# A fused attention and two-expert-layer kernel: the left tile's matmuls placed among the last steps, late value products in another PSUM bank, and a new written-out order

## The chip, the cores and the metric

The kernel runs on one core of one Trainium2 chip. The time is the device time of one execution in microseconds (us); of the kernel before there are three runs, with a median of 684.05 us (683.52 to 684.1). One further execution was profiled. The core's engines are TensorE (PE, with its weight loads as PEld), VectorE (DVE), ScalarE (ACT), GpSimd (POOL) and SyncE (SP), which issues most DMAs; each takes its instructions in order, and semaphores order them against one another.

## What is computed

Three stages follow one another; the output of each is the input of the next (cut from the reference):

```python
# 1. attention: q, k, v of shape (4, 8, 576, 64), window 64
scores = q @ k^T / sqrt(64); masked to 0 <= i - j < 64; softmax; @ v
x = attn_out.transpose(0, 2, 1, 3).reshape(2304, 512)
# 2. dense layer: w_in (512, 2048), w_out (2048, 512)
h = x @ w_in
g = np.where(h >= 1, h, np.where(h <= -1, 0.0, (h + 1) ** 2 / 4))
x = g @ w_out
# 3. eight experts, one for each token: w1[e] (512, 1024), w2[e] (1024, 512)
logits = x @ w_gate
expert_idx = np.argmax(logits, axis=1)
out[t] = gate_w[t] * (np.maximum(x[t] @ w1[e], 0.0) @ w2[e])   # e = expert_idx[t]
```

gate_w is the largest softmax probability of a token. All is float32.

## The kernel before

A float32 matmul is done as three: each operand is split into a high and a low part (hi, lo), and hi*hi, hi*lo and lo*hi are added up in PSUM. The 2304 tokens are 18 tiles of 128.

**Phase 1** runs through five blocks of 3, 4, 4, 4 and 3 tiles, with 16 steps for each (steps 0 to 79). A step takes 128 of the 2048 hidden columns: layer 1 (`h<-xT,wi`, L590) into an h bank, the clipped square and its split on ScalarE, VectorE and GpSimd (L601 to L614), layer 2 (`acc<-wo`, L634) added up in four acc banks. The attention of later chunks of tokens is done between these steps: scores (`S<-qk`, L388) into S, mask and exponentials, transposes (L458), and value products (`av<-pb,vt`, L473), which `both_parts` places in an acc bank for the first two blocks and in S afterwards. S is one buffer of two banks; h has two banks, each its own buffer. The profile writes down each attention matmul of the order as two records, so that 16 of the order are 32 there.

**Phase 2** (steps 80 to 119) treats one expert, the commonest of the first tile, as the main one and applies it to all tokens, in five blocks of four tiles (two in the last) with eight steps each. L590 and L634 serve here too, with the expert's weights `we`; a relu and its split stand between them (L622, L624). When a block is done, `out_parts` scales each tile by the gate weight (L843 on VectorE or L847 on ScalarE, as the table YO_V says) and stores it (L849). The last block is tiles 16 and 17.

**The left tile.** Tokens of another expert are counted and ranked (L854 to L920), the expert is read into a register, and its weights are loaded in 16 pieces through three buffers and split (`wl<-er`, L819 to L825). Matmuls with small operands (L955) turn ranks into row numbers (`idx`, L961 to L968); GpSimd gathers the rows (`xl<-x2s,idx`, L973). TensorE transposes them (L994), applies layer 1 (`hl`, L1006), transposes the hidden rows after a relu (`hr` L1012, `ht` L1018) and applies layer 2 (`accl`, L1034). ScalarE scales the result (`yl`, L1040), and GpSimd scatters the rows over those that the main expert left in the output (L1042). If more than one left tile were needed, a loop behind would treat the rest; with these inputs it does not run.

**What sets the order.** HEAD is a list of short names, one for each piece of work (ga and gb are the layers of a phase-1 or phase-2 step, qkp and avp scores and value products of a pair of heads, hip and lop the split of the latter, zl, zh and zv loading and splitting a left weight, kg the gather, xa to xl the left tile, yo and yd scaling and storing an output tile). All engines but SyncE get their instructions in the order of this list; SyncE's order is written by hand from the same list. Tables beside it name the engine of splits and scalings that more than one engine can do.

Of the kernel before, what the change touches and what calls it, by code (L numbers as in the profile page):

```python
# [34 lines left out]
PJ_V = (0, 1, 3, 4, 8, 9, 13, 14, 16, 17, 19, 21, 25, 26, 27, 28, 29, 30, 34)  # L35
PS_V = ((15, 0), (17, 0))
# [4 lines left out]
ELO_P = (4, 6, 7, 9, 10, 14, 15)  # L41
LLO_P = (3, 4, 5, 6, 7, 8, 9, 12, 14, 15)
YO_V = ((0, 1), (1, 1), (2, 1), (2, 3), (3, 3), (4, 0), (4, 1))
# [176 lines left out]
def kernel(  # L220
# [409 lines left out]
    def layer2(acc, g, w):  # L630
        hi, lo = g
        for j, (ga, wa) in enumerate(((hi, 0), (hi, 1), (lo, 0))):
            for t, (a, first, last) in enumerate(acc):
                nc.tensor.matmul(  # L634
                    a, ga[:, t * P:t * P + P], w[:, wa],
                    start=(first and j == 0), stop=(last and j == 2),
                )


    def take(r, t, a):  # L640

# [682 lines left out]
```

## Time and profile before

| | |
|---|---|
| median of three runs | 684.05 us |
| the profiled execution | 683.23 us |
| its span, first to last instruction | 681.5 us |
| mean granted TensorE clock | 0.997 of full speed |
| TensorE busy (matmuls) | 668.0 us, 98% |
| VectorE busy | 412.2 us, 60% |
| ScalarE busy | 390.1 us, 57% |
| GpSimd busy | 109.2 us, 16% |

A busy engine is one with an instruction in it; matmuls overlap, so TensorE's 98% says that it hardly ever stands empty, not that it could do no more. How long a group of matmuls takes is read from the start of the group to the start of the next. "Landing" of a DMA is when its data have arrived. The profiled execution's own time is 683.23 us, 1.7 above its span.

### The profile page before, as it was taken

Reading aid. Unit: us, or ns where it says so; the run is one execution under the profiler, and the core shown is the slowest. Engines: PE = TensorE matmul, PEld = TensorE weight load, DVE = VectorE, ACT = ScalarE, POOL = GpSimd, SP = SyncE. Lnnn points to the kernel's source line nnn. Section 1 sums busy time; section 2 is a strip of 40 time slices with the busy share of each in tenths; the row PEclk is TensorE's granted clock in tenths of the full one; section 3 lists DMA queues with packets and bytes.
Section 4 is the critical chain, followed back from the end, with each engine's and each line's share of the span. In section 5 each row is a group of like instructions: output and inputs, shape, how many; then the busy total and the mean of one; then the engine's idle time right before and its main releaser. Section 6 shows DMA issues by size and latency. Waiting matters only on the chain. (4 is left out here: it accounts for less than half of the span.)

```text
span 681.5 us, 11390 instructions
## 1 busy us (share of the span) xinstructions
PE 668.0 (98%) x4159; PEld 554.7 (81%) x4160; DVE 412.2 (60%) x852; ACT 390.1 (57%) x974; POOL 109.2 (16%) x91
## 2 busy tenths in 40 slices
PE   7999999999999999999999999999999999999996
PEld 3788998888888888888888899988888888888884
DVE  6999998433235423344524336889988776776431
ACT  6997888553636576455625344588555654442331
POOL 2432223112100212111111100031110000001320
PEclk9999999999999999999999999999999999999998
DMA  9996324242232333332320224354434222212441
GB/s 340 401 404 247 101 88 115 63 133 45 62 110 59 81 108 98 82 116 49 97 76 1 78 105 181 102 132 124 132 102 123 70 70 62 62 40 75 133 149 43
DMA packets 76797, 79.39 MB, mean 116 GB/s; under 512 B 46167, under 2 KB 51287, under 8 KB 76610
## 3 DMA queue, kind: packets, MB, share of 16 engines
q1 hardware_dynamic: 76578, 78.20, 37.0%
q8 instruction: 33, 0.54, 0.3%
q0 software_dynamic: 160, 0.43, 0.2%
q14 instruction: 26, 0.21, 0.1%
HBM read 53.80 MB, written 14.42 MB: 100 GB/s over the span
## 5 line engine op out<-in xcount | busy, mean ns | idle before, releaser
L590 PE MATMUL h<-xT,wi 128*128 128x512 f32 (+1 forms) x960 | 209.8, 370 | 0.7 <-DVE pb L462 0.6
L590 PEld LDWEIGHTS h<-xT,wi 128*128 128x128 f32 x960 | 174.5, 188 | 26.3 <-DVE pb L462 0.9
L634 PE MATMUL acc<-wo,ghi 128*128 128x512 f32 x576 | 146.2, 394 | 0.0
L634 PEld LDWEIGHTS acc<-wo,ghi 128*128 128x128 f32 x576 | 106.6, 188 | 22.3 <-issue 0.9
L606 DVE SCALAR_TENSOR_TENSOR a<-h,a 128x512 f32<-128x512 f32 (+1 forms) x80 | 50.7, 635 | 92.5 <-ACT a L603 92.3
L590 PE MATMUL h<-xT,we 128*128 128x512 f32 (+1 forms) x480 | 103.1, 368 | 0.0
L601 ACT ACTIVATE a<-h,half 128x512 f32<-128x512 f32 (+1 forms) x80 | 51.8, 648 | 87.9 <-PE h L590 75.7
L590 PEld LDWEIGHTS h<-xT,we 128*128 128x128 f32 x480 | 84.2, 188 | 15.3
L614 POOL TENSOR_TENSOR glo<-a,ghi 128x512 fp32r<-128x512 f32 (+1 forms) x37 | 46.6, 1262 | 255.7 <-ACT ghi L612 223.6
L634 PE MATMUL acc<-wo,glo 128*128 128x512 f32 x288 | 78.5, 390 | 0.0
L634 PE MATMUL acc<-we,ghi 128*128 128x512 f32 x288 | 72.4, 391 | 0.0
L634 PEld LDWEIGHTS acc<-wo,glo 128*128 128x128 f32 x288 | 54.1, 188 | 11.6
L634 PEld LDWEIGHTS acc<-we,ghi 128*128 128x128 f32 x288 | 53.5, 188 | 10.7
L612 ACT ACTIVATE ghi<-a 128x512 fp32r<-128x512 f32 (+1 forms) x80 | 46.2, 585 | 24.4 <-PE acc L634 14.9
L734 DVE TENSOR_TENSOR gpr<-xg,wgb 128x1024 f32<-128x1024 f32 x34 | 44.2, 1301 | 17.3 <-ACT gpr L742 15.9
L726 DVE CUSTOM_DVE_ANT_0 junk<-xg,wgb 128x512 bf16<-128x512 f32 x76 | 54.0, 711 | 0.8
L742 ACT ACTIVATE gpr<-gpr 128x512 f32<-128x512 f32 x68 | 39.9, 586 | 23.2 <-DVE gpr L734 22.7
L622 ACT ACTIVATE ghi<-h 128x512 fp32r<-128x512 f32 (+1 forms) x40 | 22.0, 551 | 47.8 <-PE h L590 37.8
L603 ACT ACTIVATE a<-a 128x512 f32<-128x512 f32 (+1 forms) x80 | 47.0, 589 | 1.1
L614 DVE TENSOR_TENSOR glo<-a,ghi 128x512 fp32r<-128x512 f32 (+1 forms) x43 | 26.7, 625 | 25.4 <-ACT ghi L612 22.3
L634 PE MATMUL acc<-we,glo 128*128 128x512 f32 x144 | 39.2, 389 | 0.0
L624 DVE SCALAR_TENSOR_TENSOR glo<-h,ghi 128x512 fp32r<-128x512 f32 (+1 forms) x40 | 25.2, 632 | 20.4 <-ACT ghi L622 19.9
(167 smaller groups left out, 746.7 us busy)
## 6 DMA issues: line engine op xcount, KB each, us to landing
qk<-in_qq_dram SPq DMA_DIRECT2D x26, 320.0 KB, 3.5
er<-in_w_dram SPq DMA_DIRECT2D x32, 256.0 KB, 2.9
wraw<-in_wi_dram SPq DMA_DIRECT2D x14, 512.0 KB, 7.9
wraw<-in_wo_dram SPq DMA_DIRECT2D x14, 512.0 KB, 8.0
vt<-in_vv_dram SPq DMA_DIRECT2D x26, 256.0 KB, 3.6
xg<-x2s SPq DMA_DIRECT2D x18, 256.0 KB, 2.9
out_dram<-y SPq DMA_DIRECT2D x18, 256.0 KB, 2.4
x2s<-xrow SPq DMA_DIRECT2D x8, 512.0 KB, 3.2
```

Of the source, the lines that this page charges most:

```text
L590: nc.tensor.matmul(h[:, :n], w[:, wa, k * P:k * P + P], x[:, xa, k, o:o + n], start=(i == 0), stop=(i == 3 * KD - 1),)
L601: nc.scalar.activation(a[:, :n], h[:, :n], ACTF.Relu, scale=0.5, bias=half[:, 0:1])
L603: nc.scalar.activation(a[:, :n], a[:, :n], ACTF.Square)
L606: nc.vector.scalar_tensor_tensor(out=a[:, :n], in0=h[:, :n], scalar=1.0, in1=a[:, :n], op0=ALU.max, op1=ALU.min)
L612: nc.scalar.activation(hi[:, :n], a[:, :n], ACTF.Copy)
L614: (nc.gpsimd if pool else nc.vector).tensor_tensor(out=lo[:, :n], in0=a[:, :n], in1=hi[:, :n].bitcast(F32), op=ALU.subtract)
L622: nc.scalar.activation(hi[:, :n], h[:, :n], ACTF.Relu)
L624: nc.vector.scalar_tensor_tensor(out=lo[:, :n], in0=h[:, :n], scalar=0.0, in1=hi[:, :n].bitcast(F32), op0=ALU.max, op1=ALU.subtract,)
L634: nc.tensor.matmul(a, ga[:, t * P:t * P + P], w[:, wa], start=(first and j == 0), stop=(last and j == 2),)
L726: nc.vector.tensor_tensor_reduce(out=junk, in0=xg[t], in1=Z["wgb"][:, e], scale=1.0, scalar=0.0, op0=ALU.mult, op1=ALU.add, accum_out=Z["L ...
L734: nc.vector.tensor_tensor(out=pr, in0=xg[t].unsqueeze(1).to_broadcast([P, 2, DM]), in1=Z["wgb"][:, e:e + 2], op=ALU.mult,)
L742: nc.scalar.activation(pr, pr, ACTF.Copy, accum_out=Z["L"][:, t, e:e + 1])
```

## The change

Three things change together.

1. The left tile's work is no longer behind the last step. Its matmuls stand between the second layers of the last block, and the scatter is issued before the last steps are done. Since the main expert's rows of tiles 16 and 17 are stored later than the scatter, the scatter would be overwritten there. So the rows of these two tiles in the output are cleared beforehand (`ez`), read back behind the scatter into `R` (`xr`, L891 of the changed kernel), and added: a tile's result is `acc * gm + R`, with `gm` the gate weight where the token belongs to the main expert and 0 where it is left (L852, L861). The last tile is added and stored in two halves of 256 columns. The last step's second layer goes tile by tile, with its last tile in two halves.
2. Value products of blocks behind the second are placed in an h bank (`both_parts`).
3. HEAD is a new list, and the engine tables are new (PJ_V, PS_V, ELO_P, LLO_P, YO_V, NRM_P, WLO_P, GLO_P, PB_V, PL_V, PP_A). TensorE has 3587 matmuls instead of 3584.

```diff
-PJ_V = (0, 1, 3, 4, 8, 9, 13, 14, 16, 17, 19, 21, 25, 26, 27, 28, 29, 30, 34)
-PS_V = ((15, 0), (17, 0))
+PJ_V = (3, 4, 5, 7, 8, 11, 18, 19, 21, 23, 27, 29, 31, 32, 33, 34)
+PS_V = ((16, 1), (17, 0), (17, 1))
...
-YO_V = ((0, 1), (1, 1), (2, 1), (2, 3), (3, 3), (4, 0), (4, 1))
+YO_V = ((0, 0), (0, 3), (1, 0), (1, 3), (3, 0))
...
-    "xh1 yd1_119 xj0 xk0 xl0 "
+    "gb116 xj0 ga118 rh117 rv117 ga119 yo3_111 xk0 rh118 gb117 yd3_111 rv118 xl0 rh119 xr1 xr0 gb118 "
+    "rv119 gb119 yo1_119 yo0_119 yd1_119 ye1_119 ys1_119 yd0_119 "
...
-        av = heads(bank("acc" if b <= TPB else "S", "av"))
+        av = heads(bank("acc" if b <= TPB else "h", "av"))
...
-    def layer2(acc, g, w):
+    def layer2(acc, g, w, by_tile):
         hi, lo = g
-        for j, (ga, wa) in enumerate(((hi, 0), (hi, 1), (lo, 0))):
-            for t, (a, first, last) in enumerate(acc):
-                nc.tensor.matmul(
-                    a, ga[:, t * P:t * P + P], w[:, wa],
-                    start=(first and j == 0), stop=(last and j == 2),
-                )
-
+        terms = ((hi, 0), (hi, 1), (lo, 0))
+        part = [(t, slice(0, DM)) for t in range(len(acc))]
+        if by_tile:
+            part[-1:] = [(len(acc) - 1, slice(o, o + DM // 2)) for o in (0, DM // 2)]
+        order = [(q, j) for j in range(3) for q in range(len(part))]
+        for q, j in sorted(order) if by_tile else order:
+            (t, cols), (ga, wa) = part[q], terms[j]
+            a, first, last = acc[t]
+            nc.tensor.matmul(
+                a[:, cols], ga[:, t * P:t * P + P], w[:, wa, cols],
+                start=(first and j == 0),
+                stop=(last and j == 2 and (not by_tile or q != len(acc) - 1)),
+            )
...
     def out_parts(j, t, a):
         ti = j * TB + t
         y = sp.tile([P, DM], F32, tag="st", name="y")
-        if (j, t) in YO_V:
+        if ti == NTILE - 1:
+            r = Z["R"].pop(ti)
+            for o in (0, DM // 2):
+                cols = slice(o, o + DM // 2)
+                nc.vector.scalar_tensor_tensor(
+                    out=y[:, cols], in0=a[:, cols], scalar=Z["gm"][:, t:t + 1], in1=r[:, cols],
+                    op0=ALU.mult, op1=ALU.add,
+                )
+                yield
+                nc.sync.dma_start(out[ti * P:ti * P + P, cols], y[:, cols])
+                yield
+            return
+        if ti in Z["R"]:
+            nc.vector.scalar_tensor_tensor(
+                out=y, in0=a, scalar=Z["gm"][:, t:t + 1], in1=Z["R"].pop(ti), op0=ALU.mult, op1=ALU.add
+            )
+        elif (j, t) in YO_V:
             nc.vector.tensor_scalar(
                 out=y, in0=a, scalar1=Z["GW"][:, ti:ti + 1], scalar2=None, op0=ALU.mult
             )
@@ -848,12 +870,33 @@
         yield
         nc.sync.dma_start(out[ti * P:ti * P + P], y)

+    LAST = TB * (NB2 - 1)
+
+    def clear_last(k):
+        nc.sync.dma_start(out[LAST * P:NT], x2s[NT:NT + 1].to_broadcast([NT - LAST * P, DM]))
+
+    def keep_parts(k):
+        n = NTILE - LAST
+        fl = Z["p2"].tile([P, n], F32, name="fl")
+        nc.vector.tensor_reduce(out=fl, in_=Z["M"][:, LAST:], axis=AX.X, op=ALU.add)
+        gm = Z["gm"] = Z["p2"].tile([P, n], F32, name="gm")
+        nc.vector.scalar_tensor_tensor(
+            out=gm, in0=fl, scalar=0.0, in1=Z["GW"][:, LAST:], op0=ALU.is_equal, op1=ALU.mult
+        )
+        yield
+
+    def read_left(t):
+        ti = LAST + t
+        r = Z["R"][ti] = Z["p2"].tile([P, DM], F32, tag="xg", name="R", bufs=2)
+        nc.sync.dma_start(r, out[ti * P:ti * P + P])
+
...
+        Z["M"] = M
...
-            g.pop(i), wout[f] if ph == 1 else W2[KF2 + f],
+            g.pop(i), wout[f] if ph == 1 else W2[KF2 + f], i == len(steps) - 1,
...
+        ("ez", once(clear_last)),
+        ("gm", keep_parts),
+        ("xr", once(read_left)),
```

Two places of TensorE and one of VectorE show what the new list moves. The first is TensorE in phase 1, a block with attention between its steps. Before (L590 layer 1, L634 layer 2, L473 value products, L388 scores):

```order
L590 MATMUL h<-xT,wi 128x512 x24
L473 MATMUL av<-pb,vt 64x64 x16
L634 MATMUL acc<-wo,ghi 128x512 x8
L634 MATMUL acc<-wo,glo 128x512 x4
L388 MATMUL S<-qk 64x128 x16
L634 MATMUL acc<-wo,ghi 128x512 x8
L634 MATMUL acc<-wo,glo 128x512 x4
L590 MATMUL h<-xT,wi 128x512 x12
```

A like stretch of the changed kernel, where layer 2 is L640:

```order
L640 MATMUL acc<-wo,ghi 128x512 x8
L640 MATMUL acc<-wo,glo 128x512 x4
L388 MATMUL S<-qk 64x128 x16
L473 MATMUL av<-pb,vt 64x64 x16
L590 MATMUL h<-xT,wi 128x512 x24
L640 MATMUL acc<-wo,ghi 128x512 x8
L640 MATMUL acc<-wo,glo 128x512 x4
L640 MATMUL acc<-wo,ghi 128x512 x8
```

Value products and scores, which had layer 2 between them, stand side by side in the second. Such pairs are 3 in TensorE's order before and 14 in the changed one.

The second place is TensorE's end. Before, from the transposes of the gathered rows (L994) to the last matmuls but those of `accl`, which follow as 8, 4, 8 and 4:

```order
L994 MATMUL tp_6783<-ct,xl 128x128 x4
L634 MATMUL acc<-we,ghi 128x512 x4
L634 MATMUL acc<-we,glo 128x512 x2
L590 MATMUL h<-xT_6163,we 128x256 x12
L634 MATMUL acc<-we,ghi 128x512 x4
L634 MATMUL acc<-we,glo 128x512 x2
L634 MATMUL acc<-we,ghi 128x512 x4
L634 MATMUL acc<-we,glo 128x512 x2
L634 MATMUL acc<-we,ghi 128x512 x4
L634 MATMUL acc<-we,glo 128x512 x2
L1006 MATMUL hl<-wl,xTl 128x512 x24
L1018 MATMUL ht<-ct,hr 128x128 x8
```

Changed, from the same transposes (L1037) on:

```order
L1037 MATMUL tp_6709<-ct,xl 128x128 x4
L590 MATMUL h<-xT_6252,we 128x256 x12
L640 MATMUL acc<-we,ghi 128x512 x4
L640 MATMUL acc<-we,glo 128x512 x2
L1049 MATMUL hl<-wl,xTl 128x512 x24
L1061 MATMUL ht<-ct,hr 128x128 x4
L640 MATMUL acc<-we,ghi 128x512 x4
L640 MATMUL acc<-we,glo 128x512 x2
L1061 MATMUL ht<-ct,hr 128x128 x4
L1077 MATMUL accl<-wl,ghl 128x512 x8
L1077 MATMUL accl<-wl,gll 128x512 x4
L590 MATMUL h<-xT_6252,we 128x256 x12
```

The left tile's layers (L1049, L1061, L1077) have moved ahead of steps 117 to 119 and of most of their second layers: behind the last row shown come six of L640, the second `accl` (8 and 4), 24 of L590 and three times the second layer.

The third place is VectorE around the row numbers of the left tile (`ia`, `is`, `idx`), which the gather needs. Before:

```order
L825 TENSOR_TENSOR wl<-er,wl 128x512
L949 TENSOR_SCALAR sel<-ct,pos 128x128 x3
L624 SCALAR_TENSOR_TENSOR glo<-h,ghi 128x256
L961 COPY ia<-ip 128x6
L962 TENSOR_TENSOR ia<-ia,ct 128x3
L964 TENSOR_REDUCE is__6650<-ia 128x2
L968 TENSOR_SCALAR idx<-is__6650 128x1
L624 SCALAR_TENSOR_TENSOR glo<-h,ghi 128x256
L825 TENSOR_TENSOR wl<-er,wl 128x512
L843 TENSOR_SCALAR y<-acc,GW 128x512
```

Changed (L831 is the split of a left weight, L865 the scaling of an output tile, L1004 to L1011 the row numbers):

```order
L624 SCALAR_TENSOR_TENSOR glo<-h,ghi 128x256
L831 TENSOR_TENSOR wl<-er,wl 128x512 x3
L865 TENSOR_SCALAR y<-acc,GW 128x512
L1004 COPY ia<-ip 128x6
L1005 TENSOR_TENSOR ia<-ia,ct 128x3
L1007 TENSOR_REDUCE is__6662<-ia 128x2
L1011 TENSOR_SCALAR idx<-is__6662 128x1
L624 SCALAR_TENSOR_TENSOR glo<-h,ghi 128x256 x2
```

Three weight splits and the scaling of an output tile now stand right ahead of the row numbers.

At the end of SyncE's order, the loads of `R` (two), the two half stores of tile 17 and the store of tile 16 follow one another; before, the last entries were three whole output tiles. At the end of VectorE's order stand the three additions: the first half of tile 17, tile 16, the second half of tile 17.

## Rows read from the trace of the kernel before

**Rows 1.** Windows: stretch, its length, then busy time (instructions) of each engine, clock, DMA.

```profile
60.00:100.00 40.00, 40.00 (x328) 35.78 (x327) 39.72 (x74) 33.33 (x78) 9.20 (x7) 1.00 0.26 83
```

**Rows 2.** Waits of TensorE from 60 us on: total, times, longest.

```profile
PE ht L1018 <- ACT hr L1012: 0.3, 1, 0.3
PE S L388 <- ACT ghi L612: 0.2, 1, 0.2
```

**Rows 3.** Timeline of TensorE, 184 to 202 us: start, busy, instruction and count.

```profile
184.91 1.98 PE L634 MATMUL acc<-wo,ghi 128*128 128x512 f32 x8
...
187.63 5.60 PE L590 MATMUL h<-xT,wi 128*128 128x512 f32 x24
193.16 1.15 PE L473 MATMUL av<-pb,vt 128*64 128x64 f32 x32
194.24 2.11 PE L634 MATMUL acc<-wo,ghi 128*128 128x512 f32 x8
...
197.19 1.10 PE L388 MATMUL S<-qk 64*64 64x128 f32 x32
198.22 2.14 PE L634 MATMUL acc<-wo,ghi 128*128 128x512 f32 x8
...
201.11 2.88 PE L590 MATMUL h<-xT,wi 128*128 128x512 f32 x12
```

**Rows 4.** Timeline of TensorE, 89 to 93 us.

```profile
89.98 1.10 PE L388 MATMUL S<-qk 64*64 64x128 f32 x32
91.01 1.15 PE L473 MATMUL av<-pb,vt 128*64 128x64 f32 x32
92.09 2.35 PE L590 MATMUL h<-xT,wi 128*128 128x384 f32 x12
```

**Rows 5.** Timeline of TensorE, 643 to 672 us.

```profile
643.96 0.23 PE L955 MATMUL ip<-info,sel 128*128 128x6 bf16 x3
...
651.14 3.04 PE L590 MATMUL h<-xT,we 128*128 128x256 f32 x24
...
655.40 0.60 PE L994 MATMUL tp<-ct,xl 128*128 128x128 f32 x4
655.76 1.17 PE L634 MATMUL acc<-we,ghi 128*128 128x512 f32 x4
...
668.22 0.60 PE L1018 MATMUL ht<-ct,hr 128*128 128x128 f32 x4
...
669.56 2.12 PE L1034 MATMUL accl<-wl,ghl 128*128 128x512 f32 x8
671.51 1.07 PE L1034 MATMUL accl<-wl,gll 128*128 128x512 f32 x4
```

**Rows 6.** Timeline of all engines, 675 to 677 us.

```profile
675.40 0.69 ACT L1040 ACTIVATE yl<-accl,is__6650 128x512 f32<-128x512 f32 x1 [5.03 <-PEq L1255]
676.36 1.00 POOL L1042 DMA_INDIRECT out_dram<-yl,idx  x1 [13.91 <-ACTq L1255]
```

**Rows 7.** DMA issues: line, engine, count, KB each, median us from issue to landing.

```profile
xg<-x2s SPq DMA_DIRECT2D x18, 256.0 KB, 2.9
out_dram<-y SPq DMA_DIRECT2D x18, 256.0 KB, 2.4
...
xl<-x2s,idx POOLq DMA_INDIRECT x1, 5.6
out_dram<-yl,idx POOLq DMA_INDIRECT x1, 3.0
```

**Rows 8.** Groups from 460 us, by shape: busy, mean ns, idle before.

```profile
L624 DVE SCALAR_TENSOR_TENSOR glo<-h,ghi 128x512 fp32r<-128x512 f32 x32 | 21.9, 685 | 13.1 <-ACT ghi L622 12.6 <-PE acc L634 0.5
...
L843 DVE TENSOR_SCALAR y<-acc,GW 128x512 f32<-128x512 f32 x7 | 5.2, 747 | 4.6 <-PE acc L634 4.2 <-ACT xj L268 0.4
...
L624 DVE SCALAR_TENSOR_TENSOR glo<-h,ghi 128x256 fp32r<-128x256 f32 x8 | 3.3, 422 | 7.3 <-ACT ghi L622 7.3
```

**Rows 9.** The last instruction of the row numbers: ns min/median/max, first and last start.

```profile
L968 DVE TENSOR_SCALAR idx<-is__6650 x1: 153/153/153, 644.8 to 644.8; 128x1 uint32<-128x1 f32 x1
```

More of the change, by code (lines that the diff above doesn't have):

```diff
@@ L40 @@
 PBB = 2
-ELO_P = (4, 6, 7, 9, 10, 14, 15)
-LLO_P = (3, 4, 5, 6, 7, 8, 9, 12, 14, 15)
-YO_V = ((0, 1), (1, 1), (2, 1), (2, 3), (3, 3), (4, 0), (4, 1))
+ELO_P = (1, 2, 3, 4, 5, 6, 7, 10, 11, 13)
+LLO_P = (1, 4, 6, 7, 8, 10, 14)
+YO_V = ((0, 0), (0, 3), (1, 0), (1, 3), (3, 0))
 SCRATCH = 4096
@@ L58 @@
 HEAD = (
[113 rows of a table removed]
-).split()
-NRM_P = (0, 1, 2, 3, 4, 5, 8, 9, 10, 15, 16, 17, 18, 19, 25, 26, 28, 30, 34, 35)
-WLO_P = (0, 2, 3, 4, 6, 20, 22, 26, 27, 28, 31)
-GLO_P = (0, 3, 4, 5, 6, 9, 13, 16, 22, 23, 25, 26, 27, 29, 34, 35, 38, 39, 40, 41, 42, 43, 46, 48, 50, 52, 53, 55, 57, 60, 61, 63, 65, 71, 77, 78, 79)
-PB_V = (0, 2, 3, 6, 7, 14, 15, 16, 18, 21, 28, 29, 31, 32, 33, 34, 35)
-PL_V = ((31, 2), (31, 3), (47, 2), (47, 3), (63, 1), (63, 2), (63, 3))
-PP_A = (15, 16, 20, 21, 24, 25, 27, 30, 31)
[113 rows of a table added]
+).split()
+NRM_P = (0, 1, 2, 3, 4, 5, 8, 9, 10, 14, 16, 17, 19, 23, 24, 27, 29, 30, 33)
+WLO_P = (0, 1, 2, 3, 4, 6, 20, 22, 26, 27, 28, 30)
+GLO_P = (0, 3, 4, 5, 6, 9, 13, 15, 17, 23, 28, 29, 30, 35, 38, 42, 43, 44, 45, 46, 48, 50, 51, 56, 57, 59, 60, 63, 64, 65, 66, 67, 68, 74)
+PB_V = (0, 2, 3, 6, 7, 14, 15, 20, 27, 34)
+PL_V = ((15, 1), (15, 2), (31, 1), (31, 2), (47, 1), (63, 0), (63, 2), (63, 3))
+PP_A = (14, 18, 20, 21, 22, 23, 27, 28, 29, 34)
 WARM = 17
@@ L691, in plane_parts @@
         yield
-    Z = {}
+    Z = {"R": {}}
     def phase2_setup():
```

223 rows, old and new, of the table HEAD are left out of this document.

## Prediction

> **What bounds the kernel now.** The windows come first: in a stretch such as 60 to 100 us TensorE is busy for all of it (40.00 of 40.00 us), beside 39.72 on VectorE and 33.33 on ScalarE [rows 1]. Next the waits of TensorE: after 60 us there are two, 0.3 us for a relu of the left tile and 0.2 us for a split of phase 1 [rows 2]. So from 60 us to its last matmul the time is TensorE's own, and a change there counts only through what TensorE issues, in which order, and what it is newly made to wait for. The timeline is read for that, from start to start, because matmuls overlap and their modelled ends do not add up.
>
> The first thing to see in it is what a short group of attention matmuls costs its neighbours. Twelve 512-column matmuls take 187.63 - 184.91 = 2.72 us, 0.227 each [rows 3]. Twenty-four ahead of value products take 193.16 - 187.63 = 5.53, against 2 x 2.72 = 5.44: going into an attention group costs 0.09. Twelve behind scores take 201.11 - 198.22 = 2.89, 0.17 over 2.72; twelve behind value products and ahead of scores take 197.19 - 194.24 = 2.95, of which 0.09 is the next entry, so 0.14 for coming out. I take 0.15 for an exit. The groups themselves take 1.08 (value products, 193.16 to 194.24) and 1.03 (scores, 197.19 to 198.22) [rows 3].
>
> The second is the end. The left tile stands behind all other matmuls: the two groups of transposes of its hidden rows take from 668.22 to 669.56, 1.34 us, where one such group elsewhere takes 655.76 - 655.40 = 0.36 [rows 5]. Behind the last matmul come the scaled copy, which starts at 675.40, and the scatter, issued at 676.36 [rows 6] with 3.0 us to its landing [rows 7], so 679.36; the span ends at 681.5, 2.1 later. Call the end of the last matmul T, 675.4 here: the scatter is issued at T+0.96 and lands at T+4.0.
>
> **The change part by part.** The sum is made against the profiled execution, 683.23 us; the median of the runs is 684.05, 0.82 above it, and I carry the difference over to the median.
>
> *Joined attention groups.* With late value products in an h bank, scores and value products no longer take the one S buffer in turn, and the new order lets them stand side by side. Counted over the two orders of TensorE, a score group and a value group touch 3 times before and 14 times after; entries from a layer's group into an attention group fall from 26 to 17, exits from 27 to 19. Where a pair stands joined already, it takes 91.01 - 89.98 = 1.03 and 92.09 - 91.01 = 1.08, what each takes alone [rows 3, 4]. So 9 entries x 0.09 = 0.8 and 8 exits x 0.15 = 1.2: -2.0. If the inner edge of a new pair cost as much as the exit that it saves, 0.8 would be left; with the 0.17 of the longer row 2.2 go. Bounds -0.8 to -2.2; I take -2.0, since the joined row shows no extra.
>
> The Trainium skill has a rule against this: the page TensorEngine Tiling (Array Packing), section Tiling Modes, says that changing the tiling mode drains TensorE. Scores (64x64 in the trace) and value products (128x64) are different modes, so by it a pair would drain inside as well. The pair at 89.98, with 1.03 and 1.08, does not show it; by the rule the sum would be 1.2 smaller, which is the first rival.
>
> *The left tile among the last steps.* Its second transposes no longer stand right behind the relu that feeds them; the second layer of one expert step, six matmuls x 0.227 = 1.36 us, lies between, more than covering the 0.3 [rows 2]. The 1.34 become two groups of 0.36 to 0.4: -0.55. There is now a second way out of transposes into 512-column work; the way out into the left tile's second layer costs 671.51 - 669.56 = 1.95 for eight, where 8 x 0.227 = 1.82: +0.13 [rows 5]. Together -0.4, bounds -0.6 to 0.
>
> *By halves.* The last three 512-column matmuls become six of 256. In the last steps 24 matmuls of 256 columns and six of 512 take 655.40 - 651.14 = 4.26 [rows 5]; without 1.36 for the six that is 0.12 each, so 0.72 against 0.68: +0.04. The first half starts no earlier for it, since its add waits on VectorE for TensorE's very last matmul.
>
> *The tail.* Scatter, read and add are new in series. Behind the left tile's last matmul TensorE still has 4.26 + 2 x 1.36 = 7.0 us of work. With the 0.96 of before, the scatter is issued at T-6.0 and lands 3.0 later, T-3.0. Two reads of 256 KB, a load that takes 2.9 at the median (xg) [rows 7], issued one after the other some 0.35 apart, land at T-0.1 and T+0.25. VectorE then adds two halves and a whole tile, 0.42 + 0.68 + 0.42 by its like operation on 256 and 512 columns [rows 8]: T+1.6. The store of the last part is issued by T+2.0 and lands in 2.4 (y) [rows 7], T+4.4. Against T+4.0 before: +0.4. If the reads and stores are 0.4 quicker in the empty queues of the end, nothing: bounds 0 to +0.6, and I take +0.2. The clearing store of zeros is issued at step 81 of 120 and nothing needs it soon: 0. The mask of kept tokens is two small VectorE operations off the path: 0.
>
> *What TensorE may newly wait for.* The gather of the left rows moves forward with the left tile. Before, the last index matmuls start at 643.96, the index is done at 644.95 [rows 5, 9], the gather takes 5.6 [rows 7], and the transposes stand at 655.40: some 4 us of cover. After, VectorE computes the index behind the scaling of a finished output tile, which waits for that tile's last matmul. From there it is 0.75 for the scaling [rows 8], 0.9 for the index and 5.6 for the gather, 7.3 in all; TensorE has three layer-1 parts and two second layers until the transposes, 1.5 x 2.9 + 2 x 1.36 = 7.1. So it waits 0.2. Bounds: 0 if the gather lands a little sooner, and several us if the scaling stands behind late weight splits (third rival). The h bank that a late value product takes is emptied by a ScalarE copy and a VectorE subtraction, as that of an expert step is (0.685 for the latter [rows 8]); no row has it in an h bank, so 0 to 0.15 for each of about 15, nearer 0, because TensorE waits for no h bank where two layer-1 steps stand in a row [rows 2, 3]: +0.2. Together +0.4, bounds 0 to 3.
>
> Head: up to the first layer-1 step TensorE keeps its order and ScalarE its work, so 0.
>
> Sum: -2.0 - 0.4 + 0.04 + 0.2 + 0.4 = -1.8. That is 681.4 for a profiled execution and 684.05 - 1.8 = 682.3 on the median.
>
> **Rivals.** *A pair pays inside.* Each new pair has an inner edge that costs what an exit costs. For it: the two use the array in different shapes. Against it: the pair of rows 4. The joins then give 0.8, and the time is 683.5.
>
> *The h banks give it back.* A value product holds its bank until a subtraction that can stand behind others on VectorE, 39.72 of 40.00 busy early on [rows 1]; the next layer-1 part waits. At 0.15 for each of 15 that is 2.2 instead of 0.2, so 684.3. Against it: the two short waits are all that TensorE has after 60 us [rows 2].
>
> *The left tile comes too early (slower).* Its index, gather and weight splits are the one chain that the change pulls forward. If the three weight splits ahead of the scaling on VectorE wait for their loads, then the index, the gather and the transposes all slide, and TensorE, which takes matmuls in order, stands still; by the sum above nothing covers this path. It decides from 3.2 us of lateness (1.8, and 1.4 for 0.2% of the time). One load of 256 KB that is awaited in full costs 2.9 [rows 7], two in a row 5.8; I price it at 4: 686.3. For it: no row has this order. Against it: in the trace TensorE never waits for a left weight or for the gather [rows 2].
>
> *Better still.* No new wait, and a quiet tail: 682.3 - 0.8 = 681.5.
>
> **How the numbers follow.** About 0.2% (1.4 us) is what a measurement can tell from no change: faster means below 682.7, slower above 685.4. Chances: the forecast 0.44, a pair pays inside 0.19, the h banks 0.13, the left tile too early 0.15, better still 0.09. Faster: 0.37 of the forecast's 0.44, all of better still, and 0.02 of the first rival, 0.48. Slower: the third rival and 0.04 of the second, 0.19. The same: 0.33. The range leaves out the far end of the slower case: 681.0 to 685.6; the likeliest case's own is 681.7 to 683.1.
>
> **What would show it.** Right: in the timeline after, pairs of 1.03 and 1.08 with nothing at their inner edge, and twelves still at 2.72; waits of TensorE after 60 us below 1 us in sum; the left tile's transposes in two groups of about 0.4; the last store landing 4.0 to 4.4 after the last matmul. Wrong: a wait of over 1 us for the gathered rows, for a left weight or for an h bank; reads that land more than 0.5 after the last matmul, so that the adds wait for a DMA and not for TensorE; or twelves behind a joined pair at well over 2.9.

## The result, and the profile after

The changed kernel takes 687.74 us in the median of six runs (686.92 to 688.24), the kernel before 683.46 beside it: 1.0061 times as long, with a 95% interval of 1.0049 to 1.0074. It is 4.3 us slower where 1.8 less was forecast. The profiled execution of the change is 688.24 us with a span of 686.4, 4.9 over the span of before.

The waits of TensorE after 60 us come first, in the view of [rows 2] (total, times, longest). Before, they were 0.5 us in all; now they are 3.9, and none of them names the left tile, its gather or its weights.

```profile
PE h L590 <- ACT gpr L748: 1.8, 1, 1.8
PE h L590 <- DVE a L606: 1.5, 1, 1.5
PE S L388 <- ACT sr L505: 0.6, 1, 0.6
```

The groups that the forecast had moved behave as it said. In TensorE's timeline (start, busy, instruction, count) a joined pair takes 351.68 - 350.64 = 1.04 and 352.76 - 351.68 = 1.08, as in [rows 3, 4], and the twelve behind it 355.62 - 352.76 = 2.86, an exit of 0.14.

```profile
350.64 1.10 PE L388 MATMUL S<-qk 64*64 64x128 f32 x32
351.68 1.15 PE L473 MATMUL av<-pb,vt 128*64 128x64 f32 x32
352.76 2.12 PE L640 MATMUL acc<-wo,ghi 128*128 128x512 f32 x8
...
355.62 2.88 PE L590 MATMUL h<-xT,wi 128*128 128x512 f32 x12
```

The two longest waits in the same view. Up to 342.21 TensorE stands 1.45 us for an h bank. At 486.16 it stands again, 1.85 us, and the twelve matmuls that follow take 490.35 - 486.16 = 4.19 in place of 2.72.

```profile
342.21 5.78 PE L590 MATMUL h<-xT,wi 128*128 128x512 f32 x24 [1.45 <-DVE a L606]
...
486.16 4.39 PE L590 MATMUL h<-xT,we 128*128 128x512 f32 x12 [1.85 <-ACT gpr L748]
490.35 2.24 PE L640 MATMUL acc<-we,ghi 128*128 128x512 f32 x8
```

The windows (columns as in [rows 1]) have the granted clock: 0.87 in the stretch of that wait, where the kernel before has 1.00. Between 488 and 490 us it is 0.50, the lower of the two levels (1.2 GHz); TensorE had stood still until 486.16.

```profile
480.00:490.00 10.00, 8.15 (x31) 6.10 (x30) 9.27 (x22) 7.98 (x23) 1.98 (x3) 0.87 0.46 105
...
488.00:490.00 2.00, 2.00 (x6) 1.52 (x6) 2.00 (x6) 1.75 (x5) 0.47 (x1) 0.50 1.09 176
```

What keeps the banks is seen on the in-order engines. ScalarE (ACT) has done the first piece of step 54's square (L601) at 335.36 + 0.69 = 336.05. Next in its order stands a copy of transposed probabilities, which waits 3.53 us for a DMA transpose; the second piece (L603), ready all the time, comes behind it at 340.84.

```profile
335.36 0.69 ACT L601 ACTIVATE a<-h,half 128x512 f32<-128x512 f32 x1 [2.57 <-PE h L590]
339.59 1.38 ACT L268 ACTIVATE pb<-pt 128x1024 uint16<-128x1024 uint16 x1 [3.53 <-DMA pt<-pp]
340.84 0.60 ACT L603 ACTIVATE a<-a 128x512 f32<-128x512 f32 x1
```

On VectorE (DVE) the split of step 82 (L624) runs at 480.56. ScalarE's part of step 83, the second of the two L622, is done at 479.94 + 1.08 = 481.02, but step 83's split, which gives its h bank back, stands behind four dot products and a product of the gate (L732, L740) and runs at 485.33 to 486.01; TensorE goes on at 486.16. The profile names this wait "ACT gpr"; such a piece on ScalarE ended at about the same time, 486.04. That the split is what ended it is shown by the first experiment, which moves the split alone and takes the wait away.

```profile
479.94 1.08 ACT L622 ACTIVATE ghi<-h 128x512 fp32r<-128x512 f32 x2
...
480.56 0.69 DVE L624 SCALAR_TENSOR_TENSOR glo<-h,ghi 128x512 fp32r<-128x512 f32 x1 [3.86 <-ACT ghi L622]
...
481.17 0.90 DVE L732 CUSTOM_DVE_ANT_0 junk<-xg,wgb 128x512 bf16<-128x512 f32 x1
...
483.58 0.69 DVE L732 CUSTOM_DVE_ANT_0 junk<-xg,wgb 128x512 bf16<-128x512 f32 x1
...
484.20 1.23 DVE L740 TENSOR_TENSOR gpr<-xg,wgb 128x1024 f32<-128x1024 f32 x1
...
485.33 0.68 DVE L624 SCALAR_TENSOR_TENSOR glo<-h,ghi 128x512 fp32r<-128x512 f32 x1
```

The end, on all engines (of TensorE the last matmul alone). The scatter is issued at 673.14 and lands 3.0 later, the two reads are issued from 676.17 (the scatter's row answers to [rows 6]). The last matmul starts at 678.86 and the first addition at 679.18; the third addition ends at 680.75, and the last store, of tile 16, is issued at 681.22. The span ends at 686.4.

```profile
673.14 1.00 POOL L1085 DMA_INDIRECT out_dram<-yl,idx  x1 [16.09 <-ACT yl L1083]
...
676.17 0.81 SPq L891 DMA_DIRECT2D R<-out_dram  x2
...
678.86 0.28 PE L640 MATMUL acc<-we,glo 128*128 128x256 f32 x1
679.18 0.48 DVE L852 SCALAR_TENSOR_TENSOR y<-acc,gm,R 128x256 f32<-128x256 f32 x1 [3.30 <-PE acc L640]
679.62 0.75 DVE L861 SCALAR_TENSOR_TENSOR y<-acc,gm,R 128x512 f32<-128x512 f32 x1
679.69 1.44 SPq L857 DMA_DIRECT2D out_dram<-y  x2
680.28 0.47 DVE L852 SCALAR_TENSOR_TENSOR y<-acc,gm,R 128x256 f32<-128x256 f32 x1
681.22 0.96 SPq L871 DMA_DIRECT2D out_dram<-y  x1
```

The DMAs of the same kernel by kind (count, size of one, median us from issue to landing) show the read and the half stores at 2.9 us, and the gather at 3.6, where it took 5.6 before:

```profile
R<-out_dram SPq DMA_DIRECT2D x2, 256.0 KB, 2.9
...
out_dram<-y SPq DMA_DIRECT2D x2, 128.0 KB, 2.9
...
xl<-x2s,idx POOLq DMA_INDIRECT x1, 3.6
out_dram<-yl,idx POOLq DMA_INDIRECT x1, 3.0
```

The store of tile 16 (L871), asked for alone from 680 us on, lands 2.7 us behind its issue, so at 683.9:

```profile
DMA to landing us min/median/max: 2.7/2.7/2.7
```

From the start of the copy in [rows 6] to the end of the span it was 6.1 us; from the first addition to the end it is 7.2. Of this, the time from the last landing to the end of the span is 686.4 - 683.9 = 2.5, where it was 2.1 behind the scatter.

**Where the 4.9 us are.** From the first layer-1 matmul to the last matmul, start to start, TensorE takes 4.0 us more; the rest is the end. Added up from the starts of all matmuls, what lies over the regular pitch at entries went from 3.1 to 1.9 us and at exits from 5.4 to 4.1, together -2.5; the stall at the left tile's transposes is gone, -0.5. Against that stand three waits of 0.8, 1.6 and 2.0 (the profile's 0.6, 1.45 and 1.85, with their matmul's pitch), 1.6 of half clock, 0.35 in the head, and about 0.8 in hesitations of 0.1 us or so, whose cause the traces do not show. These are sums over the starts in the two traces and add up to 4.0 within 0.2.

### The profile page after: what moved, and what is told of

It reads as the page before. It is cut to its first block, busy times and chain, and to the rows that moved or that the text cites. A ratio compares the mean times of both kernels' runs of the same rounds, so it can differ in the third digit from the quotient of the medians.

```text
span 686.4 us, 11412 instructions
## 1 busy us (share of the span) xinstructions
PE 668.3 (97%) x4163; PEld 555.9 (81%) x4163; DVE 408.3 (59%) x849; ACT 403.2 (59%) x983; POOL 107.1 (16%) x88
## 4 chain that ended last, share of the span: by engine, by line
PE 83%; DMA 8%; ACT 4%; DVE 2%; issue 1%; SPq 1%; DVEq 0%; ACTq 0%
PE acc L640 39%; PE h L590 38%; PE av L473 2%; DMA vte<-in_vv_dram 2%; DMA er<-in_w_dram 2%; PE S L388 2%; DMA pt<-pp 2%; DMA wraw<-in_wi_dram 1%; PE accl L1077 1%; PE hl L1049 1%; DMA qqr<-in_qq_dram 1%; ACT a L601 1%; ACT a L603 1%; DVE glo L614 1%; ACT xj L268 0%
## 5 line engine op out<-in xcount | busy, mean ns | idle before, releaser
L590 PE MATMUL h<-xT,wi 128*128 128x512 f32 (+1 forms) x960 | 209.1, 370 | 2.4 <-DVE a L606 1.5
L590 PEld LDWEIGHTS h<-xT,wi 128*128 128x128 f32 x960 | 174.5, 188 | 28.6 <-DVE a L606 2.9
L640 PE MATMUL acc<-wo,ghi 128*128 128x512 f32 x576 | 145.6, 392 | 0.0
L640 PEld LDWEIGHTS acc<-wo,ghi 128*128 128x128 f32 x576 | 107.0, 188 | 21.8 <-issue 0.3
L590 PE MATMUL h<-xT,we 128*128 128x512 f32 (+1 forms) x480 | 105.2, 373 | 1.8 <-ACT gpr L748 1.8
L601 ACT ACTIVATE a<-h,half 128x512 f32<-128x512 f32 (+1 forms) x80 | 51.5, 644 | 89.4 <-PE h L590 82.7
L590 PEld LDWEIGHTS h<-xT,we 128*128 128x128 f32 x480 | 84.5, 190 | 17.7 <-issue 2.2
L640 PE MATMUL acc<-wo,glo 128*128 128x512 f32 x288 | 78.4, 390 | 0.0
L614 POOL TENSOR_TENSOR glo<-a,ghi 128x512 fp32r<-128x512 f32 (+1 forms) x34 | 42.9, 1265 | 227.3 <-ACT ghi L612 208.7
L640 PE MATMUL acc<-we,ghi 128*128 128x512 f32 x290 | 72.8, 390 | 0.0
L640 PEld LDWEIGHTS acc<-wo,glo 128*128 128x128 f32 x288 | 54.1, 188 | 11.5
L640 PEld LDWEIGHTS acc<-we,ghi 128*128 128x128 f32 x290 | 54.1, 189 | 10.9
L732 DVE CUSTOM_DVE_ANT_0 junk<-xg,wgb 128x512 bf16<-128x512 f32 x76 | 54.0, 710 | 4.0 <-DMA xg<-x2s 3.1
L603 ACT ACTIVATE a<-a 128x512 f32<-128x512 f32 (+1 forms) x80 | 46.9, 588 | 1.4
L740 DVE TENSOR_TENSOR gpr<-xg,wgb 128x1024 f32<-128x1024 f32 x34 | 42.0, 1237 | 7.9 <-ACT gpr L748 4.9
L622 ACT ACTIVATE ghi<-h 128x512 fp32r<-128x512 f32 (+1 forms) x40 | 21.7, 550 | 36.9 <-PE h L590 26.3
L624 DVE SCALAR_TENSOR_TENSOR glo<-h,ghi 128x512 fp32r<-128x512 f32 (+1 forms) x40 | 25.2, 632 | 26.5 <-ACT ghi L622 26.4
L614 DVE TENSOR_TENSOR glo<-a,ghi 128x512 fp32r<-128x512 f32 (+1 forms) x46 | 32.9, 721 | 13.5 <-ACT ghi L612 8.9
L640 PE MATMUL acc<-we,glo 128*128 128x512 f32 (+1 forms) x145 | 39.5, 388 | 0.0
```

The lines of the kernel that those rows point to most:

```text
L590: nc.tensor.matmul(h[:, :n], w[:, wa, k * P:k * P + P], x[:, xa, k, o:o + n], start=(i == 0), stop=(i == 3 * KD - 1),)
L601: nc.scalar.activation(a[:, :n], h[:, :n], ACTF.Relu, scale=0.5, bias=half[:, 0:1])
L603: nc.scalar.activation(a[:, :n], a[:, :n], ACTF.Square)
L614: (nc.gpsimd if pool else nc.vector).tensor_tensor(out=lo[:, :n], in0=a[:, :n], in1=hi[:, :n].bitcast(F32), op=ALU.subtract)
L622: nc.scalar.activation(hi[:, :n], h[:, :n], ACTF.Relu)
L624: nc.vector.scalar_tensor_tensor(out=lo[:, :n], in0=h[:, :n], scalar=0.0, in1=hi[:, :n].bitcast(F32), op0=ALU.max, op1=ALU.subtract,)
```

## Experiments

The theory after the result: the loss is order, a few ready pieces that free a bank behind others on an in-order engine, and in part the end; the joined groups are worth what was forecast. The rival: the new order is short of VectorE and ScalarE time, or the joins are paid back. The kernel before, run again beside each set of experiments, took 683.0 to 683.1 us there and 683.46 beside the change, so a difference to the change holds to about 0.4 us.

**One split moved up.** In the list, rv83 goes from behind ga84 to right behind rh83:

```diff
-rh83 dv7 tt41 pa1_79 ts39 tt32 tt43 qh9 tt34 lg6 ts38 jc0 dh14 tm44 dl11 ga84 rv83
+rh83 rv83 dv7 tt41 pa1_79 ts39 tt32 tt43 qh9 tt34 lg6 ts38 jc0 dh14 tm44 dl11 ga84
```

> The changed kernel with one name moved in the list: the split of step 83's relu on VectorE (rv83) goes from behind five dot-product pieces of the gate to right behind its ScalarE half (rh83). Theory (the loss is order: a ready piece that frees an h bank stands behind others on its in-order engine): TensorE's wait of 1.85 us at 484 goes, and with it the stretch at half clock behind it (4.39 us for twelve matmuls instead of 2.72), so 687.7 - 1.9 - 1.6 = about 684.2. Rival (VectorE is simply overloaded in this stretch, 34 of 40 us busy): the wait moves to the next step and 0 to 1 us is gained, 686.7 to 687.7.

Measured: 685.32, 1.0037 (1.0023 to 1.0051) of the kernel before; 2.4 less than the change. The wait is gone, as the theory said. Its trace has no half clock either, but this does not tell for the theory: two traces below have the wait and no half clock. The size of 3.5 us is not reached: 0.8 us of wait for the next such split (step 85, at 494) is new, and where a run has no half clock the 1.6 us for it are not there to be gained. Of its waits after 60 us:

```profile
PE h L590 <- DVE glo L624: 0.8, 1, 0.8
```

**Two copies moved back.** pb33 goes behind st55, pb19 behind exd21:

```diff
-gl52 rl54 pb33 pp32 gb52 gl53 sq54 ga55 rl55 sq55 st54 tr32 gh54 st55 ga56
+gl52 rl54 pp32 gb52 gl53 sq54 ga55 rl55 sq55 st54 tr32 gh54 st55 pb33 ga56
-lv18 pb19 ps0_15 sq26 ga27 rl27 sq27 gb24 exd21
+lv18 ps0_15 sq26 ga27 rl27 sq27 gb24 exd21 pb19
```

> The changed kernel with two names moved: the ScalarE copies of transposed probabilities (pb33, pb19), which wait for a DMA transpose, go behind the clipped-square pieces and the exponential that are ready before them. Theory (head-of-line wait on ScalarE): TensorE's waits of 1.45 us at 342 and 0.6 at 173 go, 687.7 - 2.1 = 685.6. Rival (the value products need these copies at once): the wait only changes its name, and the time stays at 687.7 or grows by up to 1.

Measured: 685.0, 1.0027 (1.0017 to 1.0037). The wait at 173 is gone, that at 341 is 0.4 instead of 1.45, and none is new; the value products did not need the copies earlier. Its profile also shows the wait of VectorE's late split with nothing behind it: TensorE stands 1.75 us, as in the change, and the twelve that follow take 486.91 - 484.09 = 2.82. So the half clock does not follow from such a wait in every execution; what decides it stays open.

```profile
484.09 2.98 PE L590 MATMUL h<-xT,we 128*128 128x512 f32 x12 [1.75 <-ACT gpr L748]
486.91 1.98 PE L640 MATMUL acc<-we,ghi 128*128 128x512 f32 x8
```

**All three.** Both edits above in one kernel: rv83, pb33 and pb19 moved.

> The changed kernel with the three names moved that the two kernels before this move apart. Theory (the loss is in three places where a ready piece stands behind a waiting one): 687.7 - 3.5 - 2.1 = 682.1, below the kernel before (683.5). Rival (the new order is short of VectorE and ScalarE time altogether): not below 685.

Measured: 684.31, 1.0017 (1.0008 to 1.0027): 3.4 less than the change, not 5.6. Two waits are left, 0.8 for step 85 and 0.7 at 340, where a copy on VectorE (pp32) turns out to wait for the same DMA transpose as pb33 did on ScalarE. The rival, not below 685, is out, but the theory's 682.1 is not reached: the losses are single places, but behind a repaired one a hidden one comes up.

**The whole tile first.** 

```diff
-yo1_119 yo0_119 yd1_119 ye1_119 ys1_119 yd0_119
+yo0_119 yd0_119 yo1_119 yd1_119 ye1_119 ys1_119
```

> The changed kernel with only the end of the list in another order: tile 16 is added and stored first, which its matmuls allow 0.7 us before the last matmul, then the two halves of tile 17; before, the first half of tile 17 headed the queue and the store of tile 16 was the last on SyncE. Theory (the tail from the last matmul to the last landing is the VectorE and SyncE queue, 0.48 + 0.75 + 0.47 us of adds and three issues): 0.7 to 1.1 us less, about 686.8. Rival (the tail is the DMA round trip from scatter to read): no change, 687.7.

Measured: 687.88, 1.0076 (1.0059 to 1.0092), no gain over the change. The first addition now waits for the second read, not for TensorE, whose last matmul starts at 676.95:

```profile
676.95 0.28 PE L640 MATMUL acc<-we,glo 128*128 128x256 f32 x1
677.73 0.75 DVE L861 SCALAR_TENSOR_TENSOR y<-acc,gm,R 128x512 f32<-128x512 f32 x1 [3.77 <-DMA R<-out_dram]
```

So the read back stands within half a microsecond of the end of the matmuls. What is added last can't be moved forward alone.

Up to its last steps this kernel has the order of the change, so its trace is a second look at it. TensorE's waits are there again (1.5, 1.0 and 0.6 us), but without half clock: the twelve behind the longest take 488.71 - 485.86 = 2.85.

```profile
485.86 3.01 PE L590 MATMUL h<-xT,we 128*128 128x512 f32 x12 [1.52 <-ACT gpr L748]
488.71 1.98 PE L640 MATMUL acc<-we,ghi 128*128 128x512 f32 x8
```

**The left tile put back.** On the kernel with three moves, the left tile behind all steps as before, with no clearing, read or addition, and with tiles 16 and 17 scaled on VectorE as before:

```diff
-... xd0 ... xl0 rh119 xr1 xr0 gb118 rv119 gb119 yo1_119 yo0_119 yd1_119 ye1_119 ys1_119 yd0_119
+... rh119 gb118 rv119 gb119 yo0_119 xd0 yd0_119 xe0 xd1 xe1 xf0 xg0 xf1 xg1 xh0 yo1_119 xi0 xh1 yd1_119 xj0 xk0 xl0
```

> The kernel with the three moved names, and the left tile put back behind the last step as in the kernel before: its matmuls from hl on behind all others, no clearing, no read back, no addition, the last step whole; the rest of the new order and the joined groups stay. So it is the new order without the first part of the change. Theory A (read from the traces: from the last matmul to the end of the span 7.3 us with the read back against 6.1 before, and 0.5 us of stall between the transposes, less one exit of 0.13, the other way): the left tile's part of the change costs 0.8 us, so 684.3 - 0.8 = 683.5. Theory B (the prediction's sum, -0.4 + 0.04 + 0.2): undoing it costs 0.2, 684.5.

Measured: 683.08, 0.9999 (0.9990 to 1.0009) of the kernel before, and 1.2 less than with the left tile early. Theory A has the sign, but says 0.8; the prediction's sum is wrong in the sign.

**Five moves.** pp32 goes behind st54, rv85 behind rh85:

```diff
-gl52 rl54 pp32 gb52 gl53 sq54 ga55 rl55 sq55 st54 tr32
+gl52 rl54 gb52 gl53 sq54 ga55 rl55 sq55 st54 pp32 tr32
-rh85 qv9 qh14 tm52 pa2_79 ts53 ts52 dh12 pa0_79 lg8 rv85
+rh85 rv85 qv9 qh14 tm52 pa2_79 ts53 ts52 dh12 pa0_79 lg8
```

> The kernel with the three moved names and two more moved: the copy pp32 on VectorE, which waits for the same DMA transpose, goes behind step 54's square (st54), and the split of step 85 (rv85) goes right behind its ScalarE half. Theory (every wait of TensorE left between 60 us and the end is a ready piece behind a waiting or longer one): its last two waits, 0.7 and 0.8 us with some tenths around them, go, 684.3 - 1.8 = 682.5. Rival (they only hand on the lack of VectorE time): 684 or more.

Measured: 683.98, 1.0019 (1.0010 to 1.0028). Both waits are gone and one of 0.6 us for an expert's weight split is new, but the gain of 0.3 can't be told from none (with three moves the interval was 1.0008 to 1.0027). In its profile the end is late: the second addition waits for a read, whose issue SyncE had taken 1.6 us over for two. By this pair alone the theory is not shown.

**The same with the left tile last.** The two moves of the experiment before, in the kernel that has the left tile put back.

> Both: five names moved and the left tile last. Theory (the joined groups are worth 2.6 us, the left tile's move costs 0.8, and the waits were the loss): 682.5 - 0.8 = 681.7, about 1.3 us under the kernel before (683.0). Rival (the joined groups' gain is taken back by waits in any order): 683 or more.

Measured: 682.16, 0.9986 (0.9977 to 0.9995). That is 0.9 less than with three moves, and 1.8 less than with the left tile early in the same order. The kernel is a little faster than the one before, as the theory said, by 0.9 instead of 1.3.

**The reads in the order of the additions.**

```diff
-xl0 rh119 xr1 xr0 gb118
+xl0 rh119 xr0 xr1 gb118
```

(with five moves, and the end of the list as in the whole tile first).

> Five names moved, the left tile early as in the changed kernel, and the end in another order: the read of tile 16's rows is issued first, tile 16 is added and stored first, then the halves of tile 17. Theory (in the trace with the whole tile first the addition waited 0.5 us for the second read, not for TensorE, so the order of the reads has to follow): the last store is issued 0.6 us sooner than in the changed kernel, 682.5 - 0.6 = 681.9. Rival (the scatter and the read are the end of the chain in any order): 682.5 or more.

Measured: 683.29, 1.0005 (0.9996 to 1.0014): 0.7 less than with the end as in the change (683.98), where 0.6 was expected, and still 1.1 more than with the left tile last. The two numbers expected stood on 682.5 for the kernel it starts from, so they do not decide.

**Pairs taken apart.** With five moves and the left tile last, the second layer behind a pair is put between its groups, seven times:

```diff
-avp7 qkp9 rbp8 mkp9 mxp9 hip7 nmp9 gl18 lop7 rcp8 exa19 gb16
+avp7 gb16 qkp9 rbp8 mkp9 mxp9 hip7 nmp9 gl18 lop7 rcp8 exa19
```

> The kernel with five moved names and the left tile last, with seven of its eleven late pairs of scores and value products taken apart again: the second layer that followed the pair now stands between its two groups, and all else stays. Theory (a group of attention matmuls costs its neighbours 0.09 us going in and 0.15 coming out, and the inner edge of a pair nothing): 7 x 0.24 = 1.7 us more, 682.2 + 1.7 = 683.9. Rival (a pair drains inside as well, so joining saves the entry alone): 7 x 0.09 = 0.6 more, 682.8.

Measured: 684.1, 1.0016 (1.0007 to 1.0025), 1.94 more than with the pairs joined: 0.28 for a pair, where the theory has 0.24 and the rival 0.09. New waits are not the reason: TensorE's waits after 60 us are 0.7 us in its trace and 1.1 with the pairs joined. In the timeline such a place has both exits, 200.58 - 197.63 = 2.95 behind the value products (0.09 of it the next entry) and 204.51 - 201.61 = 2.90 behind the scores:

```profile
196.55 1.15 PE L472 MATMUL av<-pb,vt 128*64 128x64 f32 x32
197.63 2.11 PE L639 MATMUL acc<-wo,ghi 128*128 128x512 f32 x8
...
200.58 1.10 PE L387 MATMUL S<-qk 64*64 64x128 f32 x32
201.61 3.06 PE L589 MATMUL h<-xT,wi 128*128 128x512 f32 x12
204.51 1.98 PE L639 MATMUL acc<-wo,ghi 128*128 128x512 f32 x8
```

The Trainium skill, page TensorEngine Tiling (Array Packing), section Tiling Modes, says that changing the tiling mode drains TensorE. At the inner edge of a joined pair no price of it shows: the pair of the change above takes 1.04 and 1.08 us, as each group does alone (1.03 and 1.08) [rows 3].

**The last waits.** With five moves and the left tile last, rh88 and rv88 go where their input is ready, zh15 and zv15 behind the relus of step 118, and the second layer of step 119 between the two groups of the left tile's transposes:

```diff
-ts61 jd2 tm62 gb86 dv15 ts63 ... rh89 rh88 qv16 gb87 rv88
+ts61 rh88 jd2 tm62 gb86 dv15 rv88 ts63 ... rh89 qv16 gb87
-gb115 zh15 zv15 ga117 gb116 ga118 rh117 rv117 ga119 yo3_111 rh118 gb117 yd3_111 rv118
+gb115 ga117 gb116 ga118 rh117 rv117 ga119 yo3_111 rh118 zh15 gb117 yd3_111 rv118 zv15
-gb118 rv119 gb119 yo0_119 xd0 yd0_119 xe0 xd1 xe1 xf0 xg0 xf1 xg1 xh0 yo1_119 xi0
+gb118 rv119 xd0 xe0 xd1 xe1 xf0 gb119 xg0 xh0 xf1 yo0_119 yd0_119 xg1 yo1_119 yd1_119 xi0
```

> The same kernel (five moved names, left tile last), with the last three waits of its trace after 60 us taken away: the split of step 88 is put where its input is ready (0.44 us of TensorE's wait at 511), the left weight's split zh15 and zv15 goes behind the relus of steps 117 and 118 (0.79 at 656), and the second layer of step 119 stands between the two groups of transposes of the left tile (0.5, less one exit of 0.15). Theory: 682.2 - 0.44 - 0.79 - 0.35 = 680.6, 0.36% under the kernel before. Rival (the waits move on, as the one of 0.8 us behind the first repair did): 681.5 or more.

Measured: 680.54, 0.9963 (0.9950 to 0.9977): 2.5 us faster than the kernel before, 7.2 faster than the change. After 60 us no wait of TensorE is left in its profile. VectorE and ScalarE are as busy in it as in the change (409.7 and 402.8 us beside 408.3 and 403.2), so the new order is not short of their time. The left tile's transposes stand in two groups of 0.36 around the second layer, and its end is that of before, scatter issued 0.96 behind the start of the copy:

```profile
664.88 0.60 PE L1060 MATMUL ht<-ct,hr 128*128 128x128 f32 x4
...
665.24 1.17 PE L639 MATMUL acc<-we,ghi 128*128 128x512 f32 x4
...
666.72 0.60 PE L1060 MATMUL ht<-ct,hr 128*128 128x128 f32 x4
...
667.07 2.09 PE L1076 MATMUL accl<-wl,ghl 128*128 128x512 f32 x8
...
672.88 0.69 ACT L1082 ACTIVATE yl<-accl,is__6657 128x512 f32<-128x512 f32 x1 [4.93 <-PEq L1300]
673.84 1.00 POOL L1084 DMA_INDIRECT out_dram<-yl,idx  x1 [23.12 <-ACTq L1300]
```

## Why the prediction was wrong

- *Joined groups, -2.0: right, and a little too small.* Entries and exits give -2.5 in the changed kernel's trace, and seven pairs are worth 1.94 on the chip. The first rival, which would have left 0.8, is out. This term and the next, -2.4 together, would put the kernel at 683.05 - 2.4 = 680.65; the last kernel, which has these two and no wait after 60 us, takes 680.54.
- *The left tile among the last steps, -0.4: right in itself.* Its transposes take 663.59 - 663.24 = 0.35 and 661.75 - 661.40 = 0.35 in TensorE's timeline after, not 1.34 [rows 5]. The last kernel gets the same gain with one second layer between them and the left tile still last.

```profile
661.40 0.60 PE L1061 MATMUL ht<-ct,hr 128*128 128x128 f32 x4
661.75 1.17 PE L640 MATMUL acc<-we,ghi 128*128 128x512 f32 x4
...
663.24 0.60 PE L1061 MATMUL ht<-ct,hr 128*128 128x128 f32 x4
663.59 2.09 PE L1077 MATMUL accl<-wl,ghl 128*128 128x512 f32 x8
```

- *The tail, +0.2: mis-sized, +1.1.* The working had the reads landing at the last matmul's end and the last store issued by T+2.0; both came so (681.22, against 679.18 for the first addition). Too low is what lies behind that: the last store landed 2.7 us after its issue instead of 2.4, T+4.7, and from there to the end of the span it is 2.5 us, where the sum carried over the 2.1 from behind the scatter. Every trace says the same: 2.5 in the seven with the read back, 2.1 in the five with the left tile last. From the start of the last matmul to the end of the span the seven take 7.5 to 8.8 us, the five 6.5 to 6.7. With the left tile last the chip gives 1.2 back in one order and 1.8 in another (1.1 against the reads in the order of the additions). So the left tile's part of the change, -0.2 in the sum, costs 1.2 to 1.8: of all terms this one had the wrong sign.
- *What TensorE may newly wait for, +0.4: the step that failed.* The text named two places, the gather and the h banks of late value products, and both stayed free of waits: the transposes of the gathered rows stand at 652.70 with none, right behind the second layers ahead of them, and the gather landed in 3.6 us, not 5.6. The waits came where the sum had no term at all, in the phase-1 and early expert steps, whose ScalarE and VectorE order the new list changes as much as TensorE's. I had taken the absence of waits [rows 2] as a property of the work, and it was one of the old order. Three waits, the half clock and the hesitations make 6.8 us there in the profiled execution, 4.4 of it the waits. Two of the waits are the prediction's own sign of being wrong, over 1 us for an h bank.

```profile
652.24 0.62 PE L640 MATMUL acc<-we,glo 128*128 128x512 f32 x2
652.70 0.60 PE L1037 MATMUL tp<-ct,xl 128*128 128x128 f32 x4
```

- *The slower rival* gave 686.3 by the left tile's chain. The time came near that, by another mechanism; there is no wait for a left weight or for the gathered rows in the trace after, and that the time came near is chance.
- *The h banks give it back* was nearest: it named VectorE's queue as what holds a bank. But it priced value products, and the banks that were late are those of layer 1; one of the two stood behind ScalarE.

What stays open: why the clock was at its lower level behind one wait of 1.85 us and not behind those of 1.75 and 1.52 in the executions of two other kernels, and where the hesitations come from. The loss does not seem to need the half clock. Two of the change's six runs, at 687.67 and 687.84 us, have a mean granted clock of 0.998, as traces without that stretch have (0.996 to 0.999), beside 0.994 in the profiled one. And the kernel with the whole tile first had no half clock in its profiled execution, which took 686.96 us. Not tested apart are the h bank of late value products and the new engine tables: every experiment keeps them, and the last one shows only that together they leave no wait after 60 us.

## What to carry to other kernels

Where one engine is busy throughout, an order that is written out by hand holds it so only piece by piece: for a new order, go through each piece that gives a buffer back, and look at what stands ahead of it on its own engine, above all a piece that waits for a DMA. Joining short groups of another matmul shape is worth what their edges cost, read from the start of the group behind them. Work that is moved off the end by a write and a read back has to save more than the read's landing and the extra stores: here it cost 1.1 to 1.8 us, and moving one piece of other work into the stall gave the gain without it.

## What the runs showed that I had not expected

The issue of one DMA on SyncE is about 0.35 us as a rule (the median of the 18 output stores before), but where three follow one another at the end one took 0.96. The gather of 128 rows landed in 5.6 us in one kernel and 3.6 in the other. The span ends 2.1 us after the last landing where that is GpSimd's scatter, and 2.5 where it is a store of SyncE; no run shows why.
